# A decode attention kernel on one core: P*V's diagonal picked by a VectorE mask, heads normalised once at the end, x loaded as rows

## The chip, the cores and the metric

The kernel runs on 1 core of one Trainium2 chip. The metric is device time in microseconds (us), the median of several executions. On one core a run is called fast unless it lies over 1.5% above the fastest of its kernel.

## The reference, cut to what matters

Two independent decode attentions, A and B, share shapes: one query token, 32 heads of 128, no grouping of heads. A attends over all 16384 keys, B over the last 4096. All tensors are bf16.

```python
def _A_ref(x, k_cache, v_cache, wq, wo):          # x: 1x1x512, caches: 1x32x16384x128
    q = (x @ wq)...                               # wq: 512x4096 -> 32 heads of 128
    scores = einsum("bhqd,bhkd->bhqk", q, k) * (128 ** -0.5)
    p = softmax(scores)
    o = einsum("bhqk,bhkd->bhqd", p, v)
    return o.reshape(1, 1, 4096) @ wo             # wo: 4096x512
# _B_ref: the same on k_cache[:, :, 12288:], v_cache[:, :, 12288:]
# result: concatenate([a, b], axis=-1)            # 1x1x1024
```

Each key and each value is used once. A's K and V are 134 MB each, B's 34 MB each, and the four weights 4.2 MB each: 352 MB to read for very little arithmetic.

## The kernel before

K tiles are 128 partitions x 256 keys x 128 (64 KB per partition, 8.4 MB). There are 16 such loads for A (two heads each) and 4 for B (eight heads each, in two *units* of four heads). Two K buffers and one V buffer fill SBUF. Every load goes out on one queue, SP, as soon as its buffer is released; this is the `_Loads` list.

Scores are made on VectorE, one chunk of 64 keys at a time: `_mult` multiplies the K tile in place by q, `_add` adds the two halves of each key, TensorE (`_red`, multiplied by an identity) sums in PSUM, VectorE reduces the last eight (`_softmax`), ScalarE exponentiates. The probabilities of a partition belong to one head of the unit; the others in its row are exactly zero.

P*V then runs as matmuls over four keys at once. That gives four keys' probabilities against four keys' values: only the blocks with equal key index e are wanted, the diagonal of a 4x4 block pattern.

```python
def _pv(nc, cx, u):
    u.csum = ...                                        # VectorE: sum of exp per partition and head
    acc = cx.acc[cx.turn]                               # PSUM, 128 x 512 f32, two of them in turn
    for t in range(T):
        r = 32 * (t % 4)
        cx.o(nc.tensor.matmul(acc[r : r + 4 * R, :],
            lhsT=ch.p[:, t % (U // 4), :, :],           # 4 keys x R heads
            rhs=u.load.vt[:, k : k + 4, :],             # 4 keys x 128
            start=(t < 4), stop=(t >= T - 4)))
    if u is u.load.units[-1]:
        cx.loads.release(u.load.v_tag)                  # the V buffer is free: next V load goes out
    cx.o(nc.scalar.copy(u.acc_sb[:, :], acc[:, :]))     # ScalarE: PSUM -> SBUF

def _fin_fold(nc, cx, u):                               # TensorE picks the diagonal
    cx.o(nc.tensor.matmul(u.f_ps[0:R, DH : DH + 1], lhsT=u.csum[:, :], rhs=cx.ones_col[:, 0:1], ...))
    for e in range(4):
        cx.o(nc.tensor.matmul(u.f_ps[0:R, 0:DH], lhsT=cx.sel[:, e, 0:R],
                              rhs=u.acc_sb[:, e * DH : (e + 1) * DH], ...))

def _fin_row(nc, cx, u):                                # per unit: 1/sum, scale
    cx.o(nc.vector.reciprocal(recip[0:R, :], u.f_ps[0:R, DH : DH + 1]))
    cx.o(nc.scalar.activation(out=u.orow[0:R, :], in_=u.f_ps[0:R, 0:DH], func=ACT.Copy, scale=recip))

def _fin_col(nc, cx, u):                                # 4 small matmuls put the heads in columns
    ...

    # main loop (cut): fin_pe runs _fin_fold / _fin_col, fin_dve runs _fin_row
    for i, x in enumerate(loads):
        for c, ch in enumerate(x.chunks):
            _mult(nc, cx, ch)
            if prev is not None:
                _softmax(nc, cx, prev)
            fin_pe()
            _add(nc, cx, ch)
            fin_dve()                                   # VectorE stands here in program order
            _red(nc, cx, ch)
            if i and c == min(i - 1, 2):
                pv(loads[i - 1])
            prev = ch
```

x is loaded transposed, four 2-byte elements per partition, on the ACT queue. At the end `_out` multiplies by wo: A first, then B in five pieces that follow the last loads (wo B comes in pieces of 2048, 1024, 512, 256 and 256 KB).

The softmax here doesn't subtract the row's maximum and nothing guards it: scores larger than these inputs give would overflow.

## Time and profile before

| | before |
|---|---|
| time, median of 4 runs | 826.50 us (826.38 to 826.56) |
| span of the profiled run | 824.8 us |
| bytes on the SP queue | 352.33 MB, 99.0% of 16 engines' span |
| busy: TensorE / VectorE / ScalarE | 400.4 / 583.0 / 98.8 us |

First the page's head: busy time of the engines, then the DMA rows of the 40 slices, then the queue table. A digit is the busy share of a slice in tenths.

```profile
span 824.8 us, 5931 instructions
PE 400.4 (49%) x2448; PEld 152.1 (18%) x2448; DVE 583.0 (71%) x307; ACT 98.8 (12%) x441; POOL 1.2 (0%) x8
...
DMA  9999999999999999999999999999999999999997
...
q1 hardware_dynamic: 8212, 352.33, 99.0%
q8 instruction: 19, 0.31, 0.2%
...
q10 hardware_dynamic: 288, 0.00, 0.0%
```

No compute engine is near full, and the DMA engines are never below 9 but at the end. q8 carries instructions, q10 is x. The windows view of the same kernel from 40 to 800 us shows, after the busy times, the granted clock, the DMA share and GB/s:

```profile
40.00:800.00 760.00, 369.89 (x2206) 137.19 (x2207) 577.30 (x287) 92.36 (x430) 0.00 (x0) 0.67 1.00 432
```

A share of 1.00 at 432 GB/s for 760 us. The Trainium skill, "DMA: Bandwidth & Descriptors", section Specifications, gives a fabric ceiling of 435 GB/s, and this trace is within 1% of it. (The same table's 358 GB/s per core is a limit for two cores that share HBM; one core alone is not held to it here.)

The chain of waits could mislead. It ends in DMA, but puts a quarter on VectorE, because it follows, for each load, what released its buffer:

```profile
DMA 57%; DVE 24%; PE 13%; issue 4%; ACT 1%; another core or an unknown queue 1%; SPq 0%; ACTq 0%; DVEq 0%
```

The view of who waited for whom shows VectorE's own two large waits (total us, times, longest):

```profile
DVE kt L163 <- DMA kt<-in_A_k_cache_dram: 118.1, 14, 22.7
DVE recip L258 <- PE f_ps L247: 90.5, 21, 10.5
```

VectorE waits 118.1 us for K, 22.7 of them before the first K tile. It also waits 90.5 us, standing at the reciprocal, until P*V, ScalarE's copy and the fold have ended. One such moment in the timeline (start, length, what; in brackets the idle time before it and what ended it):

```profile
784.47 4.58 PE L226 MATMUL acc<-vt,p_sb 128*8 128x512 bf16 x48
...
789.16 0.59 ACT L236 COPY acc_sb<-acc 128x512 f32<-128x512 f32 x1 [13.57 <-PE acc L226]
...
789.80 1.04 PE L247 MATMUL f_ps<-acc_sb,sel 128*2 128x128 f32 x8 [0.73 <-ACT acc_sb L236]
...
790.87 0.16 DVE L258 RECIPROCAL recip<-f_ps 2x1 f32<-2x1 f32 x1 [7.34 <-PE f_ps L247]
```

Finally TensorE's timeline of the tail. L226 is the last P*V, L292 is x wo, first for A, then for B:

```profile
802.10 3.42 PE L226 MATMUL acc<-vt,p_sb 128*16 128x512 bf16 x32 [5.61 <-DMA vt<-in_B_v_cache_dram]
...
808.53 5.32 PE L292 MATMUL out<-wo_t,ocA 128*1 128x256 bf16 x64 [0.28 <-DVE ocA L287]
816.76 1.91 PE L292 MATMUL out<-wo_t,ocB 128*1 128x256 bf16 x32 [2.91 <-DMA wo_t<-in_B_wo_dram]
...
821.75 0.38 PE L292 MATMUL out<-wo_t,ocB 128*1 128x256 bf16 x4 [0.25 <-DMA wo_t<-in_B_wo_dram]
```

Output B waits for wo, piece by piece. TensorE stands idle for 2.9 us between output A and the first piece of wo B. In the last 2.2 us of these output B is ready to start (its first weights were loaded at 814.5), so the compute ahead of it has at least 2.2 us to spare.

### The profile page before, as it was taken

The page shows a single profiled execution, that of the slowest core. Times are in us where ns is not written, and L with a number is a line of the kernel's source. Part 1 is how long each engine was busy: PE and PEld are TensorE (multiplying, and loading weights), DVE is VectorE, ACT ScalarE, POOL GpSimd, SP SyncE. Part 2 cuts the span into 40 slices and gives each one's busy share as a digit, 9 for nine tenths or more (in the row PEclk, how much of TensorE's full clock was granted, in tenths as well). Part 3 has the DMA queues.
Part 4 walks back from the last instruction along what each step waited for, and adds up shares of the span by engine and source line. Part 5 has one row for each costly group of instructions (what it writes and reads, how often), then busy time and mean ns, then how long its engine had stood idle before and what let it go on. Part 6 is the DMA issues. An engine that isn't in the chain of part 4 may idle for free.

```text
span 824.8 us, 5931 instructions
## 1 busy us (share of the span) xinstructions
PE 400.4 (49%) x2448; PEld 152.1 (18%) x2448; DVE 583.0 (71%) x307; ACT 98.8 (12%) x441; POOL 1.2 (0%) x8
## 2 busy tenths in 40 slices
PE   3435554456255626265436345365616372535566
PEld 1111211122022202021112111122202121212123
DVE  2099895987469867789194959598556878598900
ACT  1000101111111101011111101101101110101120
POOL 0000000000000000000000000000000000000000
PEclk9856867575677668685767576757658575867578
DMA  9999999999999999999999999999999999999997
GB/s 381 432 458 408 454 411 452 416 446 436 416 454 417 449 420 443 429 428 443 415 444 429 433 432 432 436 418 448 423 424 438 445 418 448 417 429 436 427 423 293
DMA packets 8527, 352.71 MB, mean 428 GB/s; under 512 B 1202, under 2 KB 1204, under 8 KB 1588
## 3 DMA queue, kind: packets, MB, share of 16 engines
q1 hardware_dynamic: 8212, 352.33, 99.0%
q8 instruction: 19, 0.31, 0.2%
q14 instruction: 8, 0.07, 0.0%
q10 hardware_dynamic: 288, 0.00, 0.0%
HBM read 352.32 MB, written 0.00 MB: 427 GB/s over the span
## 4 chain that ended last, share of the span: by engine, by line
DMA 57%; DVE 24%; PE 13%; issue 4%; ACT 1%; another core or an unknown queue 1%; SPq 0%; ACTq 0%; DVEq 0%
DMA kt<-in_A_k_cache_dram 43%; DVE kt L163 13%; DVE kt L172 9%; DMA vt<-in_A_v_cache_dram 7%; PE red L182 6%; PE acc L226 6%; DMA vt<-in_B_v_cache_dram 4%; DMA wo_t<-in_B_wo_dram 4%; DVE sc L200 2%; PE f_ps L247 1%; ACT acc_sb L236 1%; SPq L112 0%; PE out L292 0%; DVE rowB L301 0%
## 5 line engine op out<-in xcount | busy, mean ns | idle before, releaser
L182 PE MATMUL red<-kt,ident 128*128 128x512 bf16 x640 | 254.5, 569 | 370.6 <-DVE kt L172 370.6
L163 DVE TENSOR_TENSOR kt<-kt,qallA 128x8192 bf16<-128x8192 bf16 x64 | 282.7, 4417 | 118.1 <-DMA kt<-in_A_k_cache_dram 118.1
L172 DVE TENSOR_TENSOR kt<-kt 128x4096 bf16<-128x4096 bf16 x80 | 182.2, 2278 | 0.0
L182 PEld LDWEIGHTS <-ident 128*128 128x128 bf16 x640 | 82.7, 131 | 522.2 <-issue 435.9
L226 PE MATMUL acc<-vt,p_sb 128*8 128x512 bf16 (+1 forms) x1280 | 93.3, 450 | 15.6 <-DMA vt<-in_A_v_cache_dram 10.0
L203 ACT ACTIVATE p_sb<-sc,offA 128x64 bf16<-128x64 f32 x128 | 43.5, 341 | 368.3 <-DVE sc L200 368.3
L163 DVE TENSOR_TENSOR kt<-kt,qallB 128x8192 bf16<-128x8192 bf16 x16 | 70.4, 4402 | 0.0
L258 DVE RECIPROCAL recip<-f_ps 2x1 f32<-2x1 f32 (+1 forms) x24 | 3.7, 155 | 90.5 <-PE f_ps L247 90.5
L200 DVE TENSOR_REDUCE sc<-red 128x64 f32<-128x512 f32 x80 | 54.4, 680 | 1.8 <-PE red L182 1.7
L226 PEld LDWEIGHTS <-p_sb 128*8 128x8 bf16 (+1 forms) x1280 | 34.9, 98 | 77.6 <-issue 57.7
L236 ACT COPY acc_sb<-acc 128x512 f32<-128x512 f32 x24 | 14.0, 585 | 195.7 <-PE acc L226 195.7
L203 ACT ACTIVATE p_sb<-sc,offB 128x64 bf16<-128x64 f32 x64 | 21.5, 337 | 99.9 <-DVE sc L200 99.9
L247 PE MATMUL f_ps<-acc_sb,sel 128*2 128x128 f32 (+1 forms) x192 | 24.9, 272 | 16.3 <-ACT acc_sb L236 16.3
L203 ACT ACTIVATION_READ_ACCUMULATOR p_sb<-sc,offA 128x1 f32 x128 | 24.0, 187 | 0.0
L127 PE MATMUL q_ps<-wq_t,scr 128*128 128x512 bf16 x64 | 15.9, 411 | 14.2 <-DMA wq_t<-in_A_wq_dram 13.2
L247 PEld LDWEIGHTS f_ps<-acc_sb,sel 128*2 128x2 f32 (+1 forms) x192 | 14.4, 85 | 22.1 <-ACT acc_sb L236 18.7
L203 ACT ACTIVATION_READ_ACCUMULATOR p_sb<-sc,offB 128x1 f32 x64 | 12.0, 187 | 0.0
L260 ACT ACTIVATE orow<-f_ps,recip 2x128 bf16<-2x128 f32 (+1 forms) x24 | 8.6, 358 | 20.0 <-DVE recip L258 15.7
L127 PEld LDWEIGHTS <-scr 128*128 128x128 bf16 x64 | 6.6, 104 | 23.0 <-DVE scr L99 8.7
L273 PE MATMUL oc_ps<-orow,place 2*128 2x32 bf16 (+1 forms) x96 | 6.3, 176 | 0.7 <-ACT orow L260 0.7
L99 DVE COPY scr<-xTB 128x128 bf16<-128x128 bf16 x4 | 0.7, 318 | 8.2 <-DMA xTB<-in_B_x_dram 8.2
L273 PEld LDWEIGHTS <-place 2*128 2x128 bf16 (+1 forms) x96 | 4.0, 93 | 12.2 <-issue 12.2
(32 smaller groups left out, 40.1 us busy)
## 6 DMA issues: line engine op xcount, KB each, us to landing
kt<-in_B_k_cache_dram SPq DMA_DIRECT2D x8, 4096.0 KB, 40.0
vt<-in_B_v_cache_dram SPq DMA_DIRECT2D x8, 4096.0 KB, 31.6
wq_t<-in_A_wq_dram SPq DMA_DIRECT2D x1, 4096.0 KB, 12.3
wq_t<-in_B_wq_dram SPq DMA_DIRECT2D x1, 4096.0 KB
wo_t<-in_A_wo_dram SPq DMA_DIRECT2D x2, 2048.0 KB, 22.3
wo_t<-in_B_wo_dram SPq DMA_DIRECT2D x1, 2048.0 KB, 26.8
wo_t<-in_B_wo_dram SPq DMA_DIRECT2D x1, 1024.0 KB, 28.8
wo_t<-in_B_wo_dram SPq DMA_DIRECT2D x1, 512.0 KB, 29.5
```

The costliest lines, as they stand in the source:

```text
L127: cx.o(nc.tensor.matmul(q_ps[:, :], lhsT=st.xb[:, c, g, :], rhs=w[:, g, j * (512 // DH) : (j + 1) * (512 // DH), :], start=(g == 0 and c = ...
L163: cx.o(nc.vector.tensor_tensor(out=k, in0=k, in1=q.rearrange("p (o d) -> p o d", o=1).broadcast_to([P, U, DH]), op=ALU.mult,))
L172: cx.o(nc.vector.tensor_tensor(out=k[:, :, 0 : DH // 2], in0=k[:, :, 0 : DH // 2], in1=k[:, :, DH // 2 : DH], op=ALU.add,))
L182: cx.o(nc.tensor.matmul(ch.red[:, :, :], lhsT=cx.ident[:, :], rhs=ch.unit.load.kt[:, ch.k0 : ch.k0 + U, b * W : (b + 1) * W], start=(b == ...
L200: cx.o(nc.vector.tensor_reduce(out=sc[:, :], in_=ch.red[:, :, :], axis=AX.X, op=ALU.add))
L203: cx.o(nc.scalar.activation(out=ch.p[:, :, g, :], in_=sc[:, :].rearrange("p (t e) -> p t e", e=4), func=ACT.Exp, scale=SCALE, bias=u.st.of ...
L226: cx.o(nc.tensor.matmul(acc[r : r + 4 * R, :], lhsT=ch.p[:, t % (U // 4), :, :], rhs=u.load.vt[:, k : k + 4, :], start=(t < 4), stop=(t >= ...
L236: cx.o(nc.scalar.copy(u.acc_sb[:, :], acc[:, :]))
L247: cx.o(nc.tensor.matmul(u.f_ps[0:R, 0:DH], lhsT=cx.sel[:, e, 0:R], rhs=u.acc_sb[:, e * DH : (e + 1) * DH], start=False, stop=(e == 3), ski ...
L258: cx.o(nc.vector.reciprocal(recip[0:R, :], u.f_ps[0:R, DH : DH + 1]))
L260: cx.o(nc.scalar.activation(out=u.orow[0:R, :], in_=u.f_ps[0:R, 0:DH], func=ACT.Copy, scale=recip[0:R, 0:1]))
L273: cx.o(nc.tensor.matmul(cx.oc_ps[:, st.oc_at : st.oc_at + J], lhsT=cx.place[0 : u.R, at : at + P], rhs=u.orow[0 : u.R, r * J : (r + 1) * J ...
```

## The change

Its intent is to take work off TensorE and ScalarE and out of the 24 units: VectorE masks the accumulator in place in PSUM, reduces the four blocks to one, and one fold matmul adds the unit's heads into a PSUM tile with a row for every head. Sums, reciprocal, scaling and placing are then done once for all 64 heads. x comes as a row and is spread over the partitions by eight tiny matmuls.

```diff
-def _load_x(nc, cx, st, at):
+def _load_x(nc, cx, st, w):
+    nc.scalar.dma_start(out=cx.xrow[0:1, w, :], in_=st.x[0, 0:1, :])
+def _spread_x(nc, cx, st, w, at):
-    nc.scalar.dma_start(out=xT[:, :], in_=st.x[0, 0, :].rearrange("(p c) -> p c", c=KC))
+    for c in range(KC):
+        cx.o(nc.tensor.matmul(xT[:, c : c + 1], lhsT=row[:, c, :], rhs=cx.one[0:1, 0:1], ...))
 ...
 def _pv(nc, cx, u):
-    cx.o(nc.vector.tensor_reduce(out=u.csum[:, :], in_=u.cs[...], axis=AX.X, op=ALU.add))
-    cx.o(nc.scalar.copy(u.acc_sb[:, :], acc[:, :]))
+def _fin_pick(nc, cx, u):                       # where fin_dve stands
+    cx.o(nc.vector.tensor_tensor(out=acc, in0=acc,
+        in1=st.mask[:, :]...broadcast_to([P, 4, DH]), op=ALU.mult))
+    cx.o(nc.vector.tensor_reduce(out=u.s[:, :], in_=acc.rearrange("p x d -> p d x"), axis=AX.X, op=ALU.add))
 def _fin_fold(nc, cx, u):
-    (the sum's matmul and four folds into f_ps[0:R])
+    cx.o(nc.tensor.matmul(cx.f_ps[st.f_at : st.f_at + 32, 0:DH], lhsT=st.sel[:, at : at + 32],
+                          rhs=u.s[:, :], start=(u.i == 0), stop=(u.i == len(st.units) - 1), ...))
-def _fin_row, _fin_col                          # per unit
+def _fin_rows(nc, cx, sts):                     # once: sums, one reciprocal, one scaling, 8 placing matmuls
 ...
-    cx.p_poolA = pool("pA", 8)
+    cx.p_poolA = pool("pA", 7)
```

SBUF is full: the pool of A's probabilities goes from eight tiles to seven to make room.

More of the change, by code (lines that the diff above doesn't have):

```diff
@@ L85, in __init__ @@
         self.chunks = [ch for u in self.units for ch in u.chunks]
-def _load_x(nc, cx, st, at):
+def _load_x(nc, cx, st, w):
+    if w == 0:
+        cx.xrow = cx.accs_pool.tile([1, 2, st.wq.shape[0]], BF16, tag="accs", name="xrow")
+    nc.scalar.dma_start(out=cx.xrow[0:1, w, :], in_=st.x[0, 0:1, :])
+def _spread_x(nc, cx, st, w, at):
     D = st.wq.shape[0]
@@ L92, in _load_x @@
     R = st.R
-    xT = cx.singles.tile([P, KC], BF16, tag=f"xT{st.name}", name=f"xT{st.name}")
-    nc.scalar.dma_start(out=xT[:, :], in_=st.x[0, 0, :].rearrange("(p c) -> p c", c=KC))
+    xT = cx.red_pool.tile([P, KC], F32, tag="red", name="xT")
+    row = cx.xrow[0:1, w, :].rearrange("o (p c) -> o c p", c=KC)
+    for c in range(KC):
+        cx.o(nc.tensor.matmul(
+            xT[:, c : c + 1], lhsT=row[:, c, :], rhs=cx.one[0:1, 0:1], start=(c == 0), stop=(c == KC - 1),
+            skip_group_check=True,
+        ))
     n = KC * R * P
@@ L196, in _softmax @@
     R = u.R
-    if ch.i == 0:
-        u.cs = cx.cs_pool.tile([P, len(u.chunks), R], F32, tag=f"cs{u.st.name}", name="cs")
     sc = cx.sc_pool.tile([P, U], F32, tag="sc", name="sc")
@@ L208, in _softmax @@
             bias=u.st.off[:, g : g + 1],
-            accum_out=u.cs[:, ch.i, g : g + 1],
+            accum_out=u.st.cs[:, u.h0 + g, ch.i : ch.i + 1],
         ))
@@ L215, in _pv @@
     R = u.R
-    u.csum = cx.small.tile([P, R], F32, tag=f"csum{u.st.name}", name="csum")
-    cx.o(nc.vector.tensor_reduce(
-        out=u.csum[:, :], in_=u.cs[:, :, :].rearrange("p i g -> p g i"), axis=AX.X, op=ALU.add,
-    ))
     cx.turn = 1 - cx.turn
-    acc = cx.acc[cx.turn]
+    u.acc = cx.acc[cx.turn]
     T = u.st.keys // 4
@@ L226, in _pv @@
         cx.o(nc.tensor.matmul(
-            acc[r : r + 4 * R, :],
+            u.acc[r : r + 4 * R, :],
             lhsT=ch.p[:, t % (U // 4), :, :],
@@ L234, in _pv @@
         cx.loads.release(u.load.v_tag)
-    u.acc_sb = cx.accs_pool.tile([P, 4 * DH], F32, tag="accs", name="acc_sb")
-    cx.o(nc.scalar.copy(u.acc_sb[:, :], acc[:, :]))
+def _fin_pick(nc, cx, u):
+    st = u.st
+    acc = u.acc[:, :].rearrange("p (e d) -> p e d", d=DH)
+    cx.o(nc.vector.tensor_tensor(
+        out=acc, in0=acc,
+        in1=st.mask[:, :].rearrange("p (x o) -> p x o", o=1).broadcast_to([P, 4, DH]),
+        op=ALU.mult,
+    ))
+    u.s = cx.small.tile([P, DH], F32, tag="s", name="s")
+    cx.o(nc.vector.tensor_reduce(
+        out=u.s[:, :], in_=acc.rearrange("p x d -> p d x"), axis=AX.X, op=ALU.add,
+    ))
@@ L239, in _fin_fold @@
 def _fin_fold(nc, cx, u):
-    R = u.R
-    u.f_ps = cx.psf_pool.tile([8, DH + 1], F32, tag="f", name="f_ps")
+    st = u.st
+    at = st.sel_at - u.h0
     cx.o(nc.tensor.matmul(
-        u.f_ps[0:R, DH : DH + 1], lhsT=u.csum[:, :], rhs=cx.ones_col[:, 0:1],
-        start=True, stop=True, skip_group_check=True,
-    ))
-    for e in range(4):
+        cx.f_ps[st.f_at : st.f_at + 32, 0:DH],
+        lhsT=st.sel[:, at : at + 32],
+        rhs=u.s[:, :],
+        start=(u.i == 0), stop=(u.i == len(st.units) - 1), skip_group_check=True,
+    ))
@@ L247, in _fin_fold @@
+def _fin_rows(nc, cx, sts):
+    H = 32
+    csum = cx.small.tile([P, 2 * H], F32, tag="csum", name="csum")
+    for st in sts:
+        cx.o(nc.vector.tensor_reduce(
+            out=csum[:, st.f_at : st.f_at + H], in_=st.cs[:, :, :], axis=AX.X, op=ALU.add,
+        ))
         cx.o(nc.tensor.matmul(
-            u.f_ps[0:R, 0:DH],
-            lhsT=cx.sel[:, e, 0:R],
-            rhs=u.acc_sb[:, e * DH : (e + 1) * DH],
-            start=False, stop=(e == 3), skip_group_check=True,
-        ))
@@ L255, in _fin_row @@
-def _fin_row(nc, cx, u):
-    R = u.R
-    recip = cx.small.tile([8, 1], F32, tag="recip", name="recip")
-    cx.o(nc.vector.reciprocal(recip[0:R, :], u.f_ps[0:R, DH : DH + 1]))
-    u.orow = cx.small.tile([8, DH], BF16, tag="orow", name="orow")
+            cx.f_ps[st.f_at : st.f_at + H, DH : DH + 1],
+            lhsT=csum[:, st.f_at : st.f_at + H], rhs=cx.ones_col[:, 0:1],
+            start=False, stop=True, skip_group_check=True,
+        ))
+    recip = cx.small.tile([2 * H, 1], F32, tag="recip", name="recip")
@@ L260, in _fin_row @@
+    cx.o(nc.vector.reciprocal(recip[:, :], cx.f_ps[0 : 2 * H, DH : DH + 1]))
+    orow = cx.small.tile([2 * H, DH], BF16, tag="orow", name="orow")
     cx.o(nc.scalar.activation(
-        out=u.orow[0:R, :], in_=u.f_ps[0:R, 0:DH], func=ACT.Copy, scale=recip[0:R, 0:1]
+        out=orow[:, :], in_=cx.f_ps[0 : 2 * H, 0:DH], func=ACT.Copy, scale=recip[:, 0:1]
     ))
-def _fin_col(nc, cx, u):
-    st = u.st
-    J = st.wo.shape[0] // P
-    n = DH // J
-    last = u.i == len(st.units) - 1
-    for r in range(n):
-        at = cx.place_at - n * u.h0 - r
-        cx.o(nc.tensor.matmul(
-            cx.oc_ps[:, st.oc_at : st.oc_at + J],
-            lhsT=cx.place[0 : u.R, at : at + P],
-            rhs=u.orow[0 : u.R, r * J : (r + 1) * J],
-            start=(cx.oc_first and r == 0), stop=(last and r == n - 1),
-            skip_group_check=True,
-        ))
-    cx.oc_first = False
+    for st in sts:
+        J = st.wo.shape[0] // P
+        n = DH // J
+        h = st.f_at
+        for r in range(n):
+            at = cx.place_at + n * h - r
+            cx.o(nc.tensor.matmul(
+                st.oc_ps[:, 0:J],
+                lhsT=cx.place[h : h + H, at : at + P],
+                rhs=orow[h : h + H, r * J : (r + 1) * J],
+                start=(r == 0), stop=(r == n - 1),
+                skip_group_check=True,
+            ))
@@ L286, in _out @@
         st.oc = cx.singles.tile([P, J], BF16, tag=f"oc{st.name}", name=f"oc{st.name}")
-        cx.o(nc.vector.tensor_copy(st.oc[:, :], cx.oc_ps[:, st.oc_at : st.oc_at + J]))
+        cx.o(nc.vector.tensor_copy(st.oc[:, :], st.oc_ps[:, 0:J]))
     w = st.DN // 2
@@ L336 @@
     cx.accs_pool = pool("accs", 1)
-    cx.cs_pool = pool("cs", 2)
     cx.sc_pool = pool("sc", 2)
-    cx.p_poolA = pool("pA", 8)
+    cx.p_poolA = pool("pA", 7)
     cx.p_poolB = pool("pB", 4)
@@ L357, in problem @@
         st.v_view = v_cache[0, :, sk0 : sk0 + W, :]
-        st.oc_at, st.out_rows = (0, (0, 32)) if name == "A" else (64, (64, 96))
+        st.out_rows = (0, 32) if name == "A" else (64, 96)
+        st.f_at = 0 if name == "A" else 32
+        assert k_cache.shape[1] == 32
         st.p_pool = cx.p_poolA if name == "A" else cx.p_poolB
@@ L391 @@
     ld.pump()
-    at = _load_x(nc, cx, stA, 0)
-    at = _load_x(nc, cx, stB, at)
+    _load_x(nc, cx, stA, 0)
+    _load_x(nc, cx, stB, 1)
+    at = (stA.R + stB.R) * (A_wq.shape[0] // P) * P
+    cx.one = cx.singles.tile([1, 1], BF16, tag="one", name="one")
+    nc.gpsimd.memset(cx.one[:, :], 1.0)
     cx.ones_col = cx.singles.tile([P, 1], F32, tag="ones_col", name="ones_col")
     nc.gpsimd.memset(cx.ones_col[:, :], 1.0)
-    ones = cx.scr[:, at : at + 2 * P]
+    ones = cx.scr[:, at : at + 3 * P]
     nc.gpsimd.memset(ones, 1.0)
@@ L411 @@
     n_r = DH // J
-    cx.place_at = n_r * (stA.units[-1].h0) + n_r - 1
-    w = cx.place_at + P
-    cx.place = cx.singles.tile([8, 2 * P], BF16, tag="place", name="place")
+    cx.place_at = n_r - 1
+    w = cx.place_at + 2 * P
+    cx.place = cx.singles.tile([64, w], BF16, tag="place", name="place")
     nc.gpsimd.affine_select(
-        out=cx.place[:, 0:w],
-        in_=ones[0:8, 0:w],
+        out=cx.place[:, :],
+        in_=ones[0:64, 0:w],
         pattern=[[1, w]],
@@ L423 @@
     )
-    cx.sel = cx.singles.tile([P, 4, 8], F32, tag="sel", name="sel")
+    rows = cx.small.tile([P, 32], F32, tag="rows", name="rows")
     nc.vector.tensor_reduce(
-        out=cx.sel[:, :, :].rearrange("p e g -> p g e"),
-        in_=cx.ident[:, :].rearrange("p (t g e) -> p g e t", t=4, g=8),
-        axis=AX.X,
-        op=ALU.add,
-    )
+        out=rows[:, :], in_=cx.ident[:, :].rearrange("p (c w) -> p w c", w=32), axis=AX.X, op=ALU.add,
+    )
+    for st in (stA, stB):
+        H, R = 32, st.R
+        st.cs = cx.singles.tile([P, H, st.keys // U], F32, tag=f"cs{st.name}", name=f"cs{st.name}")
+        own = rows[:, 0 : 4 * R].rearrange("p (g e) -> p g e", e=4)
+        st.mask = cx.singles.tile([P, 4], F32, tag=f"mask{st.name}", name=f"mask{st.name}")
+        nc.vector.tensor_reduce(
+            out=st.mask[:, :], in_=own.rearrange("p g e -> p e g"), axis=AX.X, op=ALU.add,
+        )
+        st.sel_at = H - R
+        st.sel = cx.singles.tile([P, 2 * H - R], F32, tag=f"sel{st.name}", name=f"sel{st.name}")
+        nc.vector.memset(st.sel[:, :], 0.0)
+        nc.vector.tensor_reduce(
+            out=st.sel[:, st.sel_at : st.sel_at + R],
+            in_=own, axis=AX.X, op=ALU.add,
+        )
     for st in (stA, stB):
@@ L444 @@
     cx.turn = 0
-    cx.acc = []
-    for i in range(2):
-        cx.acc.append(cx.psout_pool.tile([P, 4 * DH], F32, tag=f"acc{i}", name=f"acc{i}"))
-        nc.vector.memset(cx.acc[i][:, :], 0.0)
-    cx.oc_ps = cx.pst_pool.tile([P, 512], F32, tag="ocp", name="oc_ps")
-    cx.oc_first = True
+    cx.acc = [
+        cx.psout_pool.tile([P, 4 * DH], F32, tag=f"acc{i}", name=f"acc{i}") for i in range(2)
+    ]
+    for acc in cx.acc:
+        nc.vector.memset(acc[:, :], 0.0)
+    cx.f_ps = cx.psf_pool.tile([P, 512], F32, tag="f", name="f_ps")
+    stA.oc_ps = cx.pst_pool.tile([P, 512], F32, tag="ocp", name="oc_ps")
+    stB.oc_ps = cx.acc[1]
     cx.out_ps = [
@@ L454 @@
     ]
+    _spread_x(nc, cx, stA, 0, 0)
+    _spread_x(nc, cx, stB, 1, stA.R * (A_wq.shape[0] // P) * P)
     _q(nc, cx, stA)
@@ L464, in fin_pe @@
         for u in fins:
-            if u.stage == 0:
+            if u.stage == 1:
                 _fin_fold(nc, cx, u)
-                u.stage = 1
-            elif u.stage == 2:
-                _fin_col(nc, cx, u)
                 u.stage = 9
@@ L474, in fin_dve @@
         for u in fins:
-            if u.stage == 1:
-                _fin_row(nc, cx, u)
-                u.stage = 2
+            if u.stage == 0:
+                _fin_pick(nc, cx, u)
+                u.stage = 1
     def pv(load):
@@ L506 @@
         fin_dve()
+    _fin_rows(nc, cx, (stA, stB))
     for p in pieces:
```

## The prediction

> **What bounds the kernel now.** The DMA engines. The page's 40 slices show DMA at 9 but for the last (7); the queue table gives the SP queue 99.0% of 16 engines' span for 352.33 MB, 428 GB/s on average. Windows from 40 to 760 us run at 430 to 435 GB/s, DMA share 1.00. The Trainium skill, "DMA: Bandwidth & Descriptors", section Specifications, states a fabric ceiling of 435 GB/s; this trace sits on it. VectorE is busy 71%, TensorE 49%, ScalarE 12%. The chain of waits names VectorE for 24%, but only as what released a load: dividing the bytes still queued by about 430 GB/s, I estimate that every load is issued 4 us or more before the engines would run dry. So compute matters only at the head and the tail.
>
> **Removed, per P*V unit (24):** the ScalarE copy of the accumulator (585 ns), eight f32 fold matmuls (272 ns each), two for the sum, four placing matmuls, csum (148 ns), the reciprocal (155 ns), orow (358 ns). TensorE about -29 us net, ScalarE about -22 us.
>
> **Added, per unit:** a VectorE multiply of 128x512 f32 in PSUM and a reduce to 128x128. The sc reduce reads as much from PSUM in 680 ns, so I estimate 1.3 to 1.4 us together: 32 us in all, less 7 removed: VectorE 583 -> about 608 us (74%). One f32 fold per unit stays.
>
> **Moved.** The pick stands where the reciprocal stood. There VectorE waited 90.5 us in all (who-waited-for-whom) for PV, copy and fold; now for PV alone. In one unit PV ended at 788.7 and the reciprocal began at 790.87 (timeline): the wait shrinks by about 2.1 us, the pick costs 1.3. So VectorE goes on no later and loads keep their slack: none of this is on the DMA's path.
>
> **Head.** x came as 8-byte pieces: 288 packets on the ACT queue, landing 7.5 and 16.8 us after issue. As rows they should land within about 5 us. But q A starts only when wq A lands (13.19), q B when wq B lands (23.04), and the next K load, issued at 30.2, is not needed until K 0 has landed at 42.3. No gain beyond at most 0.4 us for the packets (0.0% in the queue table).
>
> **Tail.** The last PV ends at 805.5; output A's matmuls ran 808.5 to 813.9; output B's then waited for wo until 816.76, and wo's last piece sets the end. The new tail (pick, fold, two sums, reciprocal, eight placing matmuls) is longer: I estimate output A at 809.8 to 815.1, ocB at 815.8, 1 us ahead of its wo. Hidden, narrowly.
>
> **Predicted: 826.2 us, range 824.4 to 827.8** (before 826.5). Chances: faster by over 2% 0.01, within 2% 0.985, slower by over 2% 0.005.
>
> **What would show it.** SP queue still 99%, 427 to 429 GB/s; VectorE 600 to 615 us, TensorE 365 to 380, ScalarE 74 to 80; x early, q still from about 13 and 23 us; the pick's wait for PV some 40 us below 90; output B still waiting for wo at about 816.8; the chain ending in DMA of wo.
>
> **What would make it wrong.** A PSUM multiply and strided reduce over 4 us dearer per unit (the loads' slack would go, and DMA share drop); A's smaller pool of probabilities (8 to 7) stalling PV; the tail over 2 us longer than estimated; or the DMA rate moving for another reason, 1% of it being 8 us.

## The result, and the profile after

The ratio of two kernels is the mean time of one's fast runs over that of the other's of the same rounds, so it is not quite the ratio of the medians.

| | before | after |
|---|---|---|
| time, median of 4 runs | 826.50 us | 826.16 us (826.13 to 826.25) |
| ratio, 95% interval | | 0.9997 (0.9983 to 1.0011) |
| span of the profiled run | 824.8 us | 824.5 us |
| busy: TensorE / VectorE / ScalarE | 400.4 / 583.0 / 98.8 us | 379.5 / 612.3 / 78.4 us |

608 fewer instructions, 20.9 us less TensorE, 20.4 us less ScalarE, 29.3 us more VectorE: and the time is the same. The head of the page after:

```profile
span 824.5 us, 5323 instructions
PE 379.5 (46%) x2180; PEld 133.0 (16%) x2180; DVE 612.3 (74%) x316; ACT 78.4 (10%) x394; POOL 1.3 (0%) x9
...
DMA  9999999999999999999999999999999999999997
...
q1 hardware_dynamic: 8212, 352.33, 99.1%
q8 instruction: 17, 0.28, 0.1%
...
q10 hardware_dynamic: 4, 0.00, 0.0%
...
DMA 51%; DVE 33%; issue 8%; PE 7%; another core or an unknown queue 1%; SPq 0%; DVEq 0%
```

The last line is the chain of waits: it now names VectorE for a third, and the time has not moved. The bytes and the SP queue's share are what they were; x is 4 packets in place of 288. The windows view from 40 to 800 us:

```profile
40.00:800.00 760.00, 348.37 (x1932) 117.86 (x1933) 603.67 (x286) 72.49 (x384) 0.00 (x0) 0.66 1.00 432
```

The busy times before the clock changed, the last two columns did not. VectorE's two large waits, and the groups of the new VectorE work (count | busy us, mean ns | idle before):

```profile
DVE kt L174 <- DMA kt<-in_A_k_cache_dram: 129.1, 14, 31.5
DVE acc L245 <- PE acc L231: 58.9, 15, 9.8
```

```profile
L245 DVE TENSOR_TENSOR acc<-acc,maskA 128x512 f32<-128x512 f32 x16 | 11.2, 698 | 28.3 <-PE acc L231 28.1
L245 DVE TENSOR_TENSOR acc<-acc,maskB 128x512 f32<-128x512 f32 x8 | 5.6, 696 | 30.8 <-PE acc L231 30.8
...
L251 DVE TENSOR_REDUCE s<-acc 128x128 f32<-128x512 f32 x24 | 16.6, 691 | 1.1
```

A pick costs 0.698 + 0.691 = 1.39 us. The wait in front of it is 31.6 us shorter than the reciprocal's was (58.9 for 90.5), which pays for the 29.3 us of work. The wait for K, less its part before the first tile, is 129.1 - 31.5 = 97.6 us, and was 118.1 - 22.7 = 95.4: VectorE has as much to spare as it had. The tail on TensorE, whose lines answer to those before:

```profile
800.55 3.37 PE L231 MATMUL acc<-vt,p_sb 128*16 128x512 bf16 x32 [7.83 <-DMA vt<-in_B_v_cache_dram]
...
807.24 5.18 PE L309 MATMUL out<-wo_t,ocA 128*1 128x256 bf16 x64 [0.25 <-DVE ocA L304]
815.24 1.91 PE L309 MATMUL out<-wo_t,ocB 128*1 128x256 bf16 x32 [2.82 <-DMA wo_t<-in_B_wo_dram]
...
821.39 0.38 PE L309 MATMUL out<-wo_t,ocB 128*1 128x256 bf16 x4 [1.42 <-DMA wo_t<-in_B_wo_dram]
```

From the start of the last P*V to that of output A it takes 6.69 us, and took 6.43: the new tail is 0.26 us longer. It is hidden as before: output B still waits 2.82 us for its first piece of wo, and 1.42 us for its last.

### The profile page after: what moved, and what is told of

It is laid out like the page before. It is cut to its first block, busy times and chain, and to the rows that moved or that the text cites. A ratio compares the mean times of both kernels' runs of the same rounds, so it can differ in the third digit from the quotient of the medians.

```text
span 824.5 us, 5323 instructions
## 1 busy us (share of the span) xinstructions
PE 379.5 (46%) x2180; PEld 133.0 (16%) x2180; DVE 612.3 (74%) x316; ACT 78.4 (10%) x394; POOL 1.3 (0%) x9
## 3 DMA queue, kind: packets, MB, share of 16 engines
q1 hardware_dynamic: 8212, 352.33, 99.1%
## 4 chain that ended last, share of the span: by engine, by line
DMA 51%; DVE 33%; issue 8%; PE 7%; another core or an unknown queue 1%; SPq 0%; DVEq 0%
DMA kt<-in_A_k_cache_dram 43%; DVE kt L174 16%; DVE kt L183 12%; PE red L193 5%; DMA vt<-in_B_v_cache_dram 4%; DMA wo_t<-in_B_wo_dram 4%; DVE sc L209 4%; PE acc L231 3%; DVE s L251 1%; DVE acc L245 1%; SPq L123 0%; PE out L309 0%; DVE rowB L318 0%; DVEq L251 0%
## 5 line engine op out<-in xcount | busy, mean ns | idle before, releaser
L193 PE MATMUL red<-kt,ident 128*128 128x512 bf16 x640 | 255.2, 570 | 400.4 <-DVE kt L183 400.1
L174 DVE TENSOR_TENSOR kt<-kt,qallA 128x8192 bf16<-128x8192 bf16 x64 | 282.7, 4417 | 129.1 <-DMA kt<-in_A_k_cache_dram 129.1
L231 PE MATMUL acc<-vt,p_sb 128*8 128x512 bf16 (+1 forms) x1280 | 90.9, 446 | 21.9 <-DMA vt<-in_A_v_cache_dram 12.8
L231 PEld LDWEIGHTS <-p_sb 128*8 128x8 bf16 (+1 forms) x1280 | 33.0, 98 | 85.3 <-issue 62.2
L245 DVE TENSOR_TENSOR acc<-acc,maskA 128x512 f32<-128x512 f32 x16 | 11.2, 698 | 28.3 <-PE acc L231 28.1
L245 DVE TENSOR_TENSOR acc<-acc,maskB 128x512 f32<-128x512 f32 x8 | 5.6, 696 | 30.8 <-PE acc L231 30.8
L251 DVE TENSOR_REDUCE s<-acc 128x128 f32<-128x512 f32 x24 | 16.6, 691 | 1.1
L309 PE MATMUL out<-wo_t,ocB 128*1 128x256 bf16 x64 | 4.3, 272 | 5.0 <-DMA wo_t<-in_B_wo_dram 5.0
L259 PE MATMUL f_ps<-s,selA 128*32 128x128 f32 x32 | 6.5, 285 | 0.0
L309 PE MATMUL out<-wo_t,ocA 128*1 128x256 bf16 x64 | 5.2, 338 | 0.3 <-DVE ocA L304 0.3
L110 DVE CAST scr<-xT 128x128 bf16<-128x128 f32 (+1 forms) x6 | 2.1, 458 | 3.7 <-PE xT L102 3.6
```

Of the source, the lines that this page charges most:

```text
L110: cx.o(nc.vector.tensor_copy(st.xb[:, :, g, :].rearrange("p c (i r) -> p r c i", r=R)[:, g, :, :], xT[:, :].rearrange("p (c o) -> p c o", ...
L174: cx.o(nc.vector.tensor_tensor(out=k, in0=k, in1=q.rearrange("p (o d) -> p o d", o=1).broadcast_to([P, U, DH]), op=ALU.mult,))
L193: cx.o(nc.tensor.matmul(ch.red[:, :, :], lhsT=cx.ident[:, :], rhs=ch.unit.load.kt[:, ch.k0 : ch.k0 + U, b * W : (b + 1) * W], start=(b == ...
L231: cx.o(nc.tensor.matmul(u.acc[r : r + 4 * R, :], lhsT=ch.p[:, t % (U // 4), :, :], rhs=u.load.vt[:, k : k + 4, :], start=(t < 4), stop=(t ...
L245: cx.o(nc.vector.tensor_tensor(out=acc, in0=acc, in1=st.mask[:, :].rearrange("p (x o) -> p x o", o=1).broadcast_to([P, 4, DH]), op=ALU.mult,))
L251: cx.o(nc.vector.tensor_reduce(out=u.s[:, :], in_=acc.rearrange("p x d -> p d x"), axis=AX.X, op=ALU.add,))
```

## The experiments

The theory: the 16 DMA engines are busy with the same bytes from start to end, so only bytes, and delays larger than the slack in front of a load, change the time. Two rivals: that the chain of waits tells what costs time (VectorE a quarter to a third of it), and that the change is slower in one part and faster in another. Twelve kernels were run, on several chips; each was timed beside the kernel before on its own chip (826.52 to 826.64 us there).

### 1. The two halves of the change

`head_only` is the kernel before with the x part of the diff alone; `pv_only` is the kernel after with x loaded as before.

```diff
# head_only, against before
-def _load_x(nc, cx, st, at):        # transposed, 128 partitions x 4
+def _load_x(nc, cx, st, w):         # a row, and _spread_x, both as in after
# pv_only, against after
-def _load_x(nc, cx, st, w):         # a row, and _spread_x
+def _load_x(nc, cx, st, at):        # as in before
```

> The kernel before with only x changed to rows spread by TensorE. Theory (the DMA engines' bytes set the time, x is not on the path): 826.2 to 826.5 us, ratio to before 0.9996 to 1.0000; x of B lands at about 8 us, q still starts at about 13.2 and 23, the second K load is still issued at about 30 us. The 0.3 us that separates after from before comes either from here (the x packets' own DMA time, 2.5 us over 16 engines, is 0.15 us) or from the P*V part. Rival (an earlier x starts everything earlier): over 1 us faster.

> The change without its x part: x in 8-byte pieces as before, P*V picked on VectorE as after. Theory: 826.2 to 826.5 us, VectorE about 612 us, ScalarE about 78 us as after. Rival (29 us more VectorE work costs time that the head gives back): slower than before by over 1 us here, and head_only faster by as much.

| run | median of 5, us | ratio to before (95%) |
|---|---|---|
| head_only | 826.41 (826.39 to 826.68) | 1.0000 (0.9988 to 1.0013) |
| pv_only | 826.41 (826.27 to 826.60) | 0.9999 (0.9987 to 1.0012) |

Neither half hides a loss of the other. VectorE is busy 583.6 us in head_only and 611.7 us in pv_only at the same time, as expected. In the packet records the 288 x packets of before took 2.46 us of one engine's time, 0.15 us when shared by 16 engines.

### 2. Two fifths of VectorE's work taken away

`half_dve` does the two large VectorE steps on half of the keys. Its output is wrong, which doesn't matter for the time. (It still passed the comparison with the reference, and so did the next run. The reference draws x, the caches and wq so small that, by my estimate from its factors, the scores are of the order of 0.0001 and the softmax is close to uniform. So the check of these two runs says nothing of their arithmetic.)

```diff
 def _mult / _add
-    k = ...kt[:, ch.k0 : ch.k0 + U, :]
+    k = ...kt[:, ch.k0 : ch.k0 + U // 2, :]
```

> After, with the two large VectorE steps (multiply by q, and the half-and-half add) on half of the keys: wrong result on purpose, same bytes. VectorE falls by about 240 us to 370. Theory (DMA engines bind): 825.5 to 826.5 us all the same. Rival (the chain of waits, which names VectorE for 33%, tells what costs time): some 80 us or more faster.

Measured: 826.13 us (825.98 to 826.33), ratio to before 0.9996 (0.9982 to 1.0009). VectorE fell from 612.3 to 361.4 us. The windows view from 40 to 800 us of half_dve, and under it its chain of waits:

```profile
40.00:800.00 760.00, 331.00 (x1932) 115.85 (x1933) 352.70 (x286) 72.44 (x384) 0.00 (x0) 0.68 1.00 432
```

```profile
DMA 78%; PE 15%; another core or an unknown queue 3%; DVE 2%; issue 1%; SPq 0%; DVEq 0%
```

After's chain named VectorE for 33%, this one for 2%, at the same time. That settles the first rival: the share of an engine in the chain was no measure of what its work costs. The freed time became waiting (196.5 us for A's K, 170.8 us for P*V).

### 3. Fewer bytes

`one_wq` loads wq once and uses it for both problems (wrong result).

```diff
-    ld.add(None, lambda: _load_wq(nc, cx, stB, 1))
+    stB.wq_t = stA.wq_t
```

> After, with wq loaded once and used for both problems: wrong result on purpose, 4.19 MB (1.19% of the bytes) less, all compute unchanged. Theory: the time falls by these bytes at 430 GB/s, 9.7 us, to 816.4 us (816 to 817). Rival (compute binds from the first K tile on): a gain only if the first K tile's earlier landing moves the whole chain, which gives the same; so this run sets the price of a byte and tells nothing against that rival alone, half_dve does.

Measured: 816.71 us (816.21 to 818.23, ratio 0.9885), 9.45 us below the median of after and 9.2 us in the span. 4.19 MB at 432 GB/s are 9.7 us. From its page:

```profile
span 815.3 us, 5323 instructions
...
q1 hardware_dynamic: 8068, 348.13, 99.0%
```

With half_dve this makes the case: 251 us of VectorE work are worth nothing, 1.2% of the bytes are worth 1.1% of the time.

### 4. How much VectorE has to give away, before and after

Dummy VectorE reduces over a constant (they measured 0.685 us each, I had put them at 0.6), n of them behind every pick, in program order; `before_n12` has them behind every reciprocal.

```diff
                 _fin_pick(nc, cx, u)        # before_n12: _fin_row(nc, cx, u)
+                _dummy(nc, cx, n)           # n = 4, 8, 12
```

> After, with 4 dummy VectorE reduces (128x512, about 0.6 us each, so 2.4 us) behind every pick: VectorE about 670 us. Theory (VectorE has 129.1 us of waits for K in after, 31.5 of them before the first K, so 97.6 us, 4.1 us per unit, to give away): still 826.0 to 826.8 us. Rival (a third of VectorE's time is on the path): some 19 us slower.

> The same with 8 dummies, 4.8 us per unit, just over the 4.1 us that VectorE can give away. Theory: the first sign of a cost, 0.7 us x 24 = 17 us, so 843 us (828 to 855), with the DMA share below 99%.

> The same with 12 dummies, 7.2 us per unit. Theory: VectorE binds now and each unit costs 3.1 us more, 75 us in all: 901 us (880 to 915), DMA share about 91%, waits for K near zero after the first.

> The kernel before with the same 12 dummies behind every reciprocal. VectorE could give away 118.1 us of waits for K there, 22.7 of them before the first K: 95.4 us, 4.0 per unit. My account of the change (the pick's 1.4 us is paid by the shorter wait for PV): within 1% of after_n12. Rival (the change puts 29 us more on VectorE, hidden only by the DMA): 20 us or more faster than after_n12.

| run | added per unit, us | median of 4, us | VectorE busy, us | SP queue's share | waits of VectorE: K / P*V or fold, us |
|---|---|---|---|---|---|
| after | 0 | 826.16 | 612.3 | 99.1% | 129.1 / 58.9 |
| after_n4 | 2.7 | 825.72 | 675.6 | 99.2% | 86.2 / 40.1 |
| after_n8 | 5.5 | 839.14 | 740.6 | 97.7% | 43.8 / 28.5 |
| after_n12 | 8.2 | 898.21 | 806.3 | 91.9% | 31.8 / 28.4 |
| before_n12 | 8.2 | 904.22 | 776.7 | 91.5% | 25.1 / 65.6 |

The first 65.6 us cost nothing; then the time bends up and the DMA share goes down. The windows view of after_n12, same stretch as before, shows the engines short of work for the first time:

```profile
40.00:800.00 760.00, 309.19 (x1720) 105.78 (x1721) 721.96 (x503) 64.38 (x340) 0.00 (x0) 0.66 0.94 402
```

VectorE's wait for K has shrunk to the one before the first tile:

```profile
DVE kt L174 <- DMA kt<-in_A_k_cache_dram: 31.8, 1, 31.8
```

The line through n = 8 and n = 12 puts the bend at about 5 us per unit, a little later than the 4.1 us I had worked out from the waits for K: the wait for P*V gives way as well, by 58.9 - 28.4 = 30.5 us, which is 1.3 us per unit more.

The packet records show the same slack from the other side. The bytes issued but not yet landed, divided by 430 GB/s, are an estimate of how long the engines can still run when a load is issued. The least of these is 6.9 us in before, 7.4 in after and 4.7 in after_n4. In after_n8 and after_n12 it is zero, three times in each.

With VectorE binding, before and after can be compared where VectorE's time counts. Were the change really 29.3 us dearer for VectorE, after_n12 would be slower by some such amount. It is 6.0 us *faster* than before_n12 (898.21 for 904.22, 0.7%), with 29.6 us more VectorE work, since VectorE waits 28.4 us at the pick and 65.6 us at the reciprocal. The waits of VectorE in the two kernels:

```profile
DVE acc L245 <- PE acc L231: 28.4, 14, 6.7
```

```profile
DVE recip L258 <- PE f_ps L247: 65.6, 21, 8.0
```

So the shorter wait pays for the pick not only on paper. after_n4 missed its expectation by 0.3 us, on the fast side; see 6.

### 5. How much the tail has to give away

Dummies ahead of the last reciprocal only.

```diff
+    _dummy(nc, cx, n)                        # n = 6, 12, in _fin_rows
     recip = cx.small.tile([2 * H, 1], F32, tag="recip", name="recip")
```

> After, with 6 dummy VectorE reduces (0.683 us each, 4.1 us) ahead of the last reciprocal only. In after's trace output B is ready 2.2 us before its first wo piece, and waits again 0.56, 0.19 and 1.42 us for the later pieces: 4.4 us of slack in all, so 4.1 us more should be hidden: 826.0 to 826.5 us, output B starting near 816.9 instead of 815.2. Rival (the tail is on the path): 830 us.

> The same with 12 dummies, 8.2 us: 4.4 us hidden, the rest not: 3.4 to 3.8 us slower than after, 829.5 to 830 us, output B no longer waiting for any wo piece.

Measured: tail_n6 825.24 us (825.04 to 825.63, ratio 0.9986, 0.9971 to 1.0001), tail_n12 829.96 us (829.42 to 830.16). 4.1 us of added work in the tail is hidden, 8.2 us shows with 3.8 us (829.96 less after's 826.16), so the tail has about 4.4 us to spare, as expected. But tail_n6 did not stay at 826.16, and missed its expected 826.0 to 826.5: it was 0.9 us *faster*. (The two were timed on different chips, where before took 826.53 and 826.50 us; their executions do not overlap.) Output B starts later and the last piece of wo is there sooner. The timeline of tail_n6:

```profile
816.54 3.44 PE L319 MATMUL out<-wo_t,ocB 128*1 128x256 bf16 x60 [0.60 <-DVE ocB L314]
820.24 0.38 PE L319 MATMUL out<-wo_t,ocB 128*1 128x256 bf16 x4 [0.27 <-DMA wo_t<-in_B_wo_dram]
```

In after the last four matmuls started at 821.39.

### 6. Where the last microsecond is

The packet records of tail_n6 and after differ in when a 16 KB instruction block was fetched, on one of the same 16 DMA engines, while the last pieces of wo were landing. I tried to move that fetch. `out_wide` makes output A from 32 matmuls of 512 columns in place of 64 of 256, 64 fewer TensorE instructions; `out_wide_refill` adds 64 back at the head, by spreading x five times.

```diff
 def _out:                                             # out_wide, for A only
-        for x in range(2): matmul(out[x], rhs=st.wo_t[:, j, x * w : (x + 1) * w], ...)
+        matmul(cx.out_ps[0][0:1, :], rhs=st.wo_t[:, j, :], ...)
 def _spread_x:                                        # out_wide_refill, besides
-    for c in range(KC):
+    for c in list(range(KC)) * 5:
```

> A version that may beat both: after, with output A as 32 matmuls of 512 columns in place of 64 of 256, so 64 fewer TensorE instructions (4218 for 4282) ahead of output B. In after a 16 KB instruction fetch of 1.10 us starts at 818.8 us, when output B is at about its 48th of 64 matmuls, and the last packet of wo ends at 820.9; in tail_n6 it started at 819.5, when wo was nearly all in, and the last packet ended at 819.6, 0.9 us of time better than after. Theory: the fetch sits on one of the 16 engines in front of its last wo packets; moved 64 instructions on it falls behind the end of wo, so 825.0 to 825.5 us, last wo packet near 819.7. Output A takes some 2 us longer but stays hidden (4.4 us of slack). Rival (tail_n6 was faster by another chance): 826.0 to 826.3 us.

> The control: out_wide with the 8 matmuls that spread x run five times (32 matmuls and 32 weight loads more at the head, same result), so again 4282 TensorE instructions, with the fetch back at the 48th matmul of output B. If the fetch's place is the cause: back to 826.0 to 826.4 us and a last wo packet near 820.9. If the 512-column form itself gains: as out_wide.

Measured: out_wide 825.22 us (824.77 to 825.97; ratio to before 0.9984, 0.9972 to 0.9997), out_wide_refill 825.11 us (824.85 to 826.28; 0.9984, 0.9971 to 0.9998). out_wide came out where it should, its control did not: it should have been back at 826. Its fetch did not go back to 818.8 us either, for output A took 8.7 us in it in place of 5.2 (I had expected 2 us more) and pushed everything behind it. In out_wide's own trace it took 9.5 us, so there too the fetch moved by this delay as well as by the instruction count. So the control does not test what it was made for. (The profiled execution of out_wide was its slowest of the five, 825.97 us.)

What all ten traces with the full set of loads and an undisturbed stream show is this, in us from the span's start. "Last V" is the start of the last P*V, which waits for it; the next columns are the end of the last large packet of wo, and the difference; then the start of the tail's last 16 KB instruction fetch, and when the store of A's row was issued:

| run | last V | wo's end | difference | fetch | A's row stored |
|---|---|---|---|---|---|
| before | 802.10 | 821.29 | 19.2 | 819.56 | 814.44 |
| head_only | 801.90 | 821.13 | 19.2 | 816.12 | 814.37 |
| after | 800.55 | 820.92 | 20.4 | 818.82 | 812.92 |
| pv_only | 800.70 | 821.00 | 20.3 | 819.12 | 813.43 |
| half_dve | 800.53 | 821.02 | 20.5 | 818.60 | 813.17 |
| after_n4 | 801.14 | 820.32 | 19.2 | 819.35 | 817.40 |
| tail_n6 | 800.43 | 819.65 | 19.2 | 819.51 | 816.45 |
| tail_n12 | 800.39 | 819.61 | 19.2 | 822.43 | 821.18 |
| out_wide | 800.41 | 819.60 | 19.2 | 820.56 | 817.89 |
| out_wide_refill | 800.39 | 819.61 | 19.2 | 819.25 | 816.76 |

Two things follow. First, every kernel with the new P*V has its last V 0.8 to 1.7 us earlier than the two with the old one. Second, in after, pv_only and half_dve the rest takes 1.1 to 1.3 us longer than in the seven others, and nearly all of the first gain is lost again. That is why after ends only 0.34 us ahead of before, and why delaying the tail, of all things, made it faster.

The packet records show where the second comes from. They hold no engine number, but an engine's packets follow one another with hardly a gap (some 0.02 us), so the last packets of each engine can be told apart. In after, 15 engines had ended their part of wo by 819.76 us. The fetch held the other one from 818.82 to 819.92. Only then did its last seven packets of wo go through, one at a time, until 820.92. pv_only shows the same with four packets (fetch until 820.20, the other engines done by 819.92), half_dve with eleven (819.62 and 819.76). Without this one engine the difference is 19.2 us in these three as well. In after_n4, and in the four kernels that delay output B (tail_n6, tail_n12, out_wide, out_wide_refill), no packet of wo starts after the fetch has ended; in before the fetch came to an engine that had just finished, and in head_only to one that ended at 820.86, ahead of the slowest (821.13). A's row was also stored before 813.5 us in exactly these three, but its store is one packet of 0.04 us, which in after was over at 816.38. So a fetch in front of an engine's last packets of wo costs 1.1 to 1.3 us here. (one_wq, not in the table, has it too: two packets, 0.7 us.)

The first is a matter of single engines too. In before one engine ended the last V at 801.60 us, all others by 800.39. In head_only two were late (801.39 and 801.14, the others by 800.18). In after all had ended by 800.06. One 32 KB packet of V takes 1.21 us, so the late engines were about one packet behind. In each of the ten kernels all engines but at most three had ended wo by some time between 819.6 and 819.9 us: what moves the end is how late the slowest of the 16 is. Why an engine falls behind before the last V is open. Fewer instruction blocks are a candidate: by the last V 18 had been fetched in before and 15 in after, each holding one engine for about 1.06 us. But in after_n4, also with 15, one engine was 0.6 us late, and no run tests it.

## Why the prediction was right, point by point

The time (826.2 predicted, 826.16 measured) and its reason, that the DMA engines bind, were right; half_dve and one_wq show it. The steps:

- **"every load is issued 4 us or more before the engines would run dry", so VectorE's extra work is free.** Right: the least estimate from the packet records is 6.9 us in before and 7.4 in after (section 4); 2.7 us more per unit cost nothing, 5.5 us cost 13 us in all.
- **The pick, 1.3 to 1.4 us.** Measured 1.39. The Trainium skill, "VectorE: DVE Perf Modes", section The TRN2 errata, has (N+151)/0.96 ns for an fp32 elementwise add, 691 ns at N = 512; the multiply here, in place in PSUM and with a broadcast mask, took 698.
- **Busy times.** VectorE 612.3 (600 to 615 predicted), TensorE 379.5 (365 to 380), ScalarE 78.4 (74 to 80): all inside, TensorE at the edge. TensorE's net saving was 20.9 us where I had said 29. By the groups, the folds, sums and placings of before took 35.8 us (24.9 + 4.6 + 6.3), and their successors 11.4, of which the folds alone 9.9: an f32 fold is two matmul instructions, and I had counted one. The rest of the gap lies in small changes of the other groups, which I did not follow up.
- **"the pick's wait for PV some 40 us below 90."** Mis-sized: 31.6 us below. I took 2.1 us saved in one unit for typical. In that unit it was 1.8: at 788.7 P*V's last matmul started, and it ended at 789.05 (784.47 + 4.58 in the timeline above). And only 15 of the 24 picks waited at all, and 21 of the reciprocals. The balance still comes out even, 31.6 us less waiting for 29.3 us more work, and before_n12 against after_n12 confirms it.
- **Head.** Right: q of A still started at 13.24 us, the last q matmul ended at 29.9 us (30.1 before), and head_only gains nothing clear of noise. "Within about 5 us" for x was wrong for B, which was used at 8.0 us (A at 2.1). x of B still had to wait its turn behind wq. The Trainium skill, "DMA: Bandwidth & Descriptors", section Queues, rings and completion order, says that an engine takes turns between queues at packet granularity; the trace agrees in part. The 1 KB of B's x went at 6.36 us, between two wq packets of 32 KB, one ending at 6.37 and the next starting at 6.40. But its load was issued at 1.36, and three wq packets of that engine came first, more than one turn; why is open.
- **Tail.** The direction was right and the size was off: I estimated output A from 809.8 to 815.1, 1.2 us later than before. Counted from the last P*V the new tail is 0.26 us longer. I had put the two sums in a row behind the fold; in the trace they run while the fold does. Output B "still waiting for wo at about 816.8" was 815.2, since the loads ended 1.5 us earlier.
- **"the DMA rate moving for another reason."** The rate did not move (432 GB/s in both), but the end of the stream did, by -1.5 us up to the last V (an engine late in before, none in after) and +1.2 us after it (the fetch in front of wo). The prediction had no term for either. They nearly cancelled: that the time fell inside the range follows from the mechanism, that it came within 0.1 us of 826.2 is luck.

## What to carry to other kernels

When the DMA engines are at a share of 1.00 and near their ceiling, ask of a change only two things: does it change the bytes, and does it delay a load's issue by more than is still queued. The share of an engine in the chain of waits does not answer the second; adding dummy work until the time bends does, and it also shows whether a change has spent slack that a later change will want. And work that takes over what its engine was waiting for is cheaper than its duration: here the pick took the place of a copy and a fold that VectorE had waited for, and 29.3 us of new VectorE work displaced 31.6 us of waiting. At the scale of 1 us in 826 the shares say nothing more; there look at the last packet of each engine.

out_wide is faster than before by 0.16% (its interval excludes 1). That it is faster than after is likely and not shown: the two were timed on different chips, and their intervals against before overlap. Its control was as fast; in both the fetch comes too late to hold up wo, so the gain fits section 6, but in the control, with the full instruction count, it can only have come by delaying output B.

## What the Trainium skill lacked or had wrong

- "Runtime: NRT & Kernel Launch", section Instruction fetch mechanics, says that instructions come in blocks of 16 KiB and that crossing a block's end is mostly hidden. The blocks agree (19 of 16 KB before, 17 after). It lacks what a block costs the data: in before and after, each of the 34 fetches ahead of the last one held one of the 16 engines (15 data packets in flight during it, 16 ahead of it) for 0.88 to 1.11 us. Where the last one fell in front of an engine's last packets of wo (after, pv_only, half_dve, one_wq), wo ended 0.7 to 1.3 us later.
- "VectorE: DVE Perf Modes" has no duration for elementwise f32 in place in PSUM or for a strided reduce from PSUM: 698 and 691 ns for 128x512 here.
- No page gives what the engines' uneven finish costs. The SP queue was busy 99.1% of after's 824.5 us, so about 817 us of each engine on average; of the other 7 us some 2 are the start and 3.5 the work after the last packet of wo, so some 2 are left for engines that end before the slowest. In before one engine ended the last V 1.2 us after all others.
